# The second layer of the third and fourth expert in high and low parts, in a three-stage kernel on one core

## The chip, the cores and the metric

The kernel runs on one core of one Trainium2 chip. The metric is the device time of one execution in microseconds (us). Inputs and outputs lie in the chip's memory; the launch is one program. An engine is named as the profile names it: PE is TensorE, DVE is VectorE, ACT is ScalarE, POOL is GpSimd, SP is SyncE.

## The reference

Three stages follow one another. Only the third is touched here.

```python
# 1: attention, 2 batches x 8 heads x 768 tokens x 64, masked by equal hash buckets
# 2: dense layer pair on the 1536 x 512 result
h = np.maximum(x @ w_in, 0.0)            # w_in 512 x 2048
x = h * h @ w_out                        # w_out 2048 x 512
# 3: eight experts with a greedy, capacity-limited assignment
logits = x @ w_gate                      # 1536 x 8
order = np.argsort(-logits.flatten())
for idx in order:                        # best (token, expert) pair first
    tok, e = idx // 8, idx % 8
    if assigned[tok] >= 0 or counts[e] >= 192: continue
    assigned[tok] = e; counts[e] += 1
for e in range(8):
    mask = assigned == e                 # 192 tokens each
    h = np.maximum(x[mask] @ w1[e], 0.0) # w1[e] 512 x 1024
    out[mask] = h @ w2[e]                # w2[e] 1024 x 512
```

All of it is in 32-bit floats. The greedy loop fixes one expert after the other: when an expert is full, its 192 tokens are known, and the remaining tokens go on.

## The kernel before

The three stages are written as lists of operations with their engine, an assumed duration, their dependencies, the buffers they take and give back, and a priority. A planner (`Sched`) puts them in one order per engine before the program is built; the order is then fixed, and each engine works through its own list from front to back. Buffers are units of named pools (`UNITS_F`), and the planner gives an operation its unit when one is free.

The third stage is `experts`. Expert number p (0 to 7) is the p-th one that the router finishes, so "the third and fourth expert" are p = 2 and p = 3. For each expert:

- the router (`rank`, `rest`, `front`, `squeeze`, `slots`) finds the 192 tokens. It is a chain of short operations on DVE and PE: comparison tables (L1342 on DVE) are counted on PE (L1349), DVE reads the counts (L1385 to L1389), PE transposes a vector twice (L1394, L1400), DVE picks the expert and its tokens, PE makes running sums (L1140, L1143) and the token list (L1468), and DVE writes the list (L1472);
- `before` gathers the tokens' rows on the POOL queue (L1647) and transposes them on PE (L1665, L1667); SP reads the expert's number and loads its weights in four parts g = 0 to 3 (L1610 a quarter of w1, L1611 a quarter of w2) into one of 12 units of the pool `raw`;
- `add1` runs the first layer of a part on PE (L1703, 8 matrix products of 192 columns) and the rectifier, on ACT or DVE;
- `add2` runs the second layer of that part. It has two forms. For p below `HP` the product is made of 32-bit numbers: 8 products of 192 columns for each part (L1744) into a transposed result, which two products with zeros have opened (L1750), which is copied out (L1803 ACT, L1805 DVE), transposed back on PE (L1812) and copied once more (L1819 ACT, L1821 DVE). For p of `HP` and above `add2r` is used: w2 and the rectified h are each split into a high part of the reduced type fp32r and the rest, and three products of parts replace the full one.

```python
nc.scalar.activation(wh(p, g, 0), w, AF.Copy)                                                   # L1621, high part of w2
nc.vector.tensor_tensor(wh(p, g, 1), w, wh(p, g, 0).bitcast(F32), op=OP.subtract)               # L1623, low part
nc.scalar.activation(h[:, :, 0:192], abank(n), AF.Relu)                                         # L1714, high part of h
nc.vector.scalar_tensor_tensor(..., 0.0, h[:, :, t].bitcast(F32), op0=OP.max, op1=OP.subtract)  # L1717, low part, two pieces
# add2r, for each of the 8 slices of 128 rows of an expert's w2, 512 columns each:
nc.tensor.matmul(o, h[:, 0:128], w, ...)      # L1772   tokens 0 to 127: high x high
nc.tensor.matmul(o, h[:, 0:128], wl, ...)     # L1773   high x low
nc.tensor.matmul(o, h[:, 256:384], w, ...)    # L1774   low x high
nc.tensor.matmul(o, h[:, 128:256], w, ...)    # L1776   tokens 128 to 191: high and low rows x high
nc.tensor.matmul(o[0:64], h[:, 128:192], wl, ...)  # L1779  high x low
```

Here the result has the tokens in its rows, so nothing is transposed back: ACT copies (L1835, L1839) and DVE adds (L1837). The split halves of w2 lie in the pool `wh`, which has two units; a part of h lies in one of three units of `hr` (`hx` for the other form). A `raw` unit goes back when its first layer is done and, for the split form, its w2 is split; for the other form when the second layer has read it. The result of an expert takes the pool `S`, which has one unit left for it. Last, POOL scatters the rows to the output (L1826).

The first layer of a part has priority 24.5, the second layer in the 32-bit form 70.5 and in the split form 20, the splits of w2 50; the smaller number goes first among what is ready.

Of the kernel before, what the change touches and what calls it, by code (L numbers as in the profile page):

```python
# [1577 lines left out]

FP = {"ga": 27, "xp": -0.5, "xe": -35.5, "m1": 24.5, "re": -38, "m2": 70.5, "ye": -30, "yt": -20, "yo": -40.5, "sc": -10.5, "sp": 50, "mr": 20}
AP = 5  # L1580
HP = 4
RSLACK, ESLACK = 0, 0.2
PSLACK = 0.15
SC = 2.2
# [8 lines left out]
def experts(tc, nc, S, ps, mem, ident, router, x2d, w1, w2, out, L, cst, slot):  # L1593
# [12 lines left out]
    def weights(p, g, v):  # L1606
# [7 lines left out]
        WD[p, g] = d = S.add("DMA", 3.7, None, [s], prio=p, lat=1.8)  # L1614
        if p < HP:
            return
# [79 lines left out]
    def add1(p, g):  # L1696
# [29 lines left out]
        T["l1", n] = a  # L1726
        if p >= HP:
            S.add("NONE", 0.0, None, [a, WS[p, g]], rel=[("raw", T["ld", p, g])])
# [8 lines left out]
    def add2(p, g):  # L1737

        n = 4 * p + g
        if p >= HP:  # L1740
            return add2r(p, g, n)
# [24 lines left out]
    def add2r(p, g, n):  # L1766

        def mm(j, b):
            w, wl = (wh(p, g, i)[:, 512 * j:512 * j + 512] for i in range(2))
            h, o, z = hx(n)[:, j], yr(p)[b], (g, j) == (3, 1)  # L1770
            if b == 0:
                nc.tensor.matmul(o, h[:, 0:128], w, start=(g == j == 0), stop=False)  # L1772
                nc.tensor.matmul(o, h[:, 0:128], wl, start=False, stop=False)  # L1773
                nc.tensor.matmul(o, h[:, 256:384], w, start=False, stop=z)  # L1774
            else:
                two = lambda: nc.tensor.matmul(o, h[:, 128:256], w, start=(g == j == 0), stop=z)  # L1776
                if not z:
                    two()
                nc.tensor.matmul(o[0:64], h[:, 128:192], wl, start=False, stop=False)  # L1779
                if z:  # L1780
                    two()

        a = T.get(("l2d", n - 1))
        js = [(j, b) for j in range(2) for b in (1, 0)] if g < 3 else [(j, b) for b in (1, 0) for j in range(2)]
        for i, (j, b) in enumerate(js):
            first = (g, i) == (0, 0)
            a = S.add("PE", MMR * (2 if b else 3), lambda j=j, b=b: mm(j, b), [WS[p, g], HD[n], a], prio=FP["mr"], acq="S" if first else (),
                      rel=[("hr", T["h", n]), ("wh", T["wh", p, g])] if i == 3 else ())
            if first:
                T["y", p] = a  # L1790
            T["l2", p, b] = a
        T["l2d", n] = a

    def after(p):
# [38 lines left out]
        def yr_ev(h):  # L1833
            if h == 0:
                nc.scalar.activation(yo(0), yr(p)[0], AF.Copy)  # L1835
            elif h == 1:
                nc.vector.tensor_tensor(yo(1), yr(p)[1][0:64], yl(), op=OP.add)  # L1837
            else:
                nc.scalar.activation(yl(), yr(p)[1][64:128], AF.Copy)  # L1839
# [5 lines left out]
        ev = []  # L1845
        if p >= HP:
            T["yl", p] = l = S.add("ACT", .6, lambda: yr_ev(2), [T["l2", p, 1]], prio=FP["yo"], acq="yl")
# [105 lines left out]
```

## Time and profile before

| what | value |
|---|---|
| median of 3 runs | 794.07 us (793.15 to 800.98) |
| the profiled execution's own time | 795.63 us |
| its span, first to last instruction | 793.9 us |
| mean granted PE clock | 0.989 of full speed |
| PE busy | 769.3 us, 97% of the span |
| DVE, ACT, POOL busy | 526.6, 414.1, 385.8 us |

Times within the trace count from the start of the span. The experts begin at about 577 us and the last scatter at 789. A matrix product of 32-bit numbers is two records of PE, since the program issues it in two passes. Durations of PE's records overlap; what a record costs PE in a dense run is the distance from one start to the next. An engine's idle time has cost only where the engine is the one that the end waits for.

### The profile page before, as it was taken

Reading aid. Unit: us, or ns where it says so; the run is one execution under the profiler, and the core shown is the slowest. Engines: PE = TensorE matmul, PEld = TensorE weight load, DVE = VectorE, ACT = ScalarE, POOL = GpSimd, SP = SyncE. Lnnn points to the kernel's source line nnn. Section 1 sums busy time; section 2 is a strip of 40 time slices with the busy share of each in tenths; the row PEclk is TensorE's granted clock in tenths of the full one; section 3 lists DMA queues with packets and bytes.
Section 4 is the critical chain, followed back from the end, with each engine's and each line's share of the span. In section 5 each row is a group of like instructions: output and inputs, shape, how many; then the busy total and the mean of one; then the engine's idle time right before and its main releaser. Section 6 shows DMA issues by size and latency. Waiting matters only on the chain.

```text
span 793.9 us, 14029 instructions
## 1 busy us (share of the span) xinstructions
PE 769.3 (97%) x5087; PEld 680.7 (86%) x5087; DVE 526.6 (66%) x1100; ACT 414.1 (52%) x825; POOL 385.8 (49%) x395
## 2 busy tenths in 40 slices
PE   8999999999988999999999999999999999999996
PEld 5788888988977889889989999998589998898885
DVE  6888988989998856733861791347967778413432
ACT  6989999999977754532442433244402312103432
POOL 2767877877896745752672473148400212311211
PEclk9999999999999999999999999999889999999999
DMA  8959648655721033310330110202265778667100
GB/s 189 235 134 197 131 104 182 136 123 128 185 73 54 1 107 107 107 53 1 107 107 1 53 54 1 80 1 81 68 220 180 249 248 282 211 226 258 41 21 20
DMA packets 87973, 94.34 MB, mean 119 GB/s; under 512 B 41920, under 2 KB 66880, under 8 KB 87904
## 3 DMA queue, kind: packets, MB, share of 16 engines
q1 hardware_dynamic: 85856, 87.16, 38.8%
q0 software_dynamic: 2048, 6.29, 2.5%
q8 instruction: 40, 0.66, 0.3%
q14 instruction: 29, 0.24, 0.1%
HBM read 63.55 MB, written 6.29 MB: 88 GB/s over the span
## 4 chain that ended last, share of the span: by engine, by line
PE 79%; issue 9%; DVE 5%; POOL 3%; ACT 2%; DMA 1%; SPq 0%; POOLq 0%; ACTq 0%; DVEq 0%
PE psTP L787 15%; PE psS L814 11%; PE psS L563 8%; PE psS L1703 8%; PE psS L1744 5%; PE psTP L599 3%; PE psO L814 3%; PE psm L814 3%; PE psTP L620 2%; PE psO L599 2%; PE psTP L621 2%; PE psm L599 2%; PE psm L620 1%; POOL out_dram L1826 1%; DVE p L611 1%
## 5 line engine op out<-in xcount | busy, mean ns | idle before, releaser
L591 POOL TENSOR_TENSOR f<-f 128x768 f32<-128x768 f32 x96 | 143.4, 1497 | 32.0 <-PE psTP L599 14.6
L800 POOL TENSOR_TENSOR r<-f,r 128x384 fp32r<-128x384 f32 x64 | 86.1, 1353 | 100.0 <-ACT r L798 95.2
L787 PE MATMUL psTP<-r 128*128 128x384 f32 x732 | 133.6, 336 | 1.1 <-DVE f L796 1.1
L787 PEld LDWEIGHTS psTP<-r 128*128 128x128 f32 x732 | 128.2, 188 | 3.8 <-DVE f L796 1.4
L796 DVE TENSOR_TENSOR f<-f,psTP 128x384 f32<-128x384 f32 x61 | 33.3, 552 | 108.3 <-ACT f L794 108.2
L814 PE MATMUL psS<-r 128*128 128x512 f32 x384 | 96.7, 396 | 0.0
L579 DVE TENSOR_REDUCE f<-psS 128x1 f32<-128x768 f32 x96 | 90.6, 947 | 5.3 <-PE psS L563 3.8
L582 ACT ACTIVATE f<-psS,f 128x768 f32<-128x768 f32 x96 | 87.0, 907 | 3.9 <-POOL f L591 1.8
L563 PE MATMUL psS<-r 128*128 128x384 f32 x384 | 87.4, 349 | 0.8 <-ACT f L582 0.8
L814 PEld LDWEIGHTS psS<-r 128*128 128x128 f32 x384 | 70.6, 188 | 13.2 <-POOL r L800 0.3
L1703 PE MATMUL psS<-ff,rf 128*128 128x192 f32 x400 | 79.6, 341 | 1.0 <-DVE rf L1707 0.9
L794 ACT ACTIVATE f<-psTP 128x384 f32<-128x384 f32 x61 | 30.1, 494 | 88.3 <-PE psTP L787 84.0
L563 PEld LDWEIGHTS psS<-r 128*128 128x128 f32 x384 | 65.2, 188 | 4.7 <-ACT f L582 1.8
L1703 PEld LDWEIGHTS psS<-ff,rf 128*128 128x128 f32 x400 | 66.7, 195 | 2.3 <-DVE rf L1707 1.6
L1826 POOL DMA_INDIRECT out_dram<-ff,ix x16 | 15.7, 982 | 100.5 <-DVE ff L1837 54.9
L1647 POOL DMA_INDIRECT ff<-x2d,ix x16 | 18.3, 1146 | 91.4 <-DVE ix L1472 67.5
L611 DVE TENSOR_TENSOR p<-psTP,p 128x384 fp32r<-128x384 f32 x102 | 55.3, 548 | 3.4 <-ACT p L607 2.6
L607 ACT ACTIVATE p<-psTP 128x384 fp32r<-128x384 f32 x102 | 49.8, 500 | 14.6 <-PE psTP L599 13.6
L599 PE MATMUL psTP<-ident,f 128*128 128x128 f32 x306 | 51.0, 278 | 1.8 <-DVE p L611 1.5
L777 POOL TENSOR_TENSOR r<-f,r 128x1024 fp32r<-128x1024 f32 x16 | 40.5, 2530 | 23.3 <-ACT r L775 23.3
L798 ACT ACTIVATE r<-f 128x384 fp32r<-128x384 f32 x64 | 33.2, 527 | 27.0 <-DVE f L796 27.0
L599 PEld LDWEIGHTS psTP<-ident,f 128*128 128x128 f32 x306 | 38.8, 143 | 8.0 <-issue 2.1
(411 smaller groups left out, 1630.2 us busy)
## 6 DMA issues: line engine op xcount, KB each, us to landing
rf<-in_moe_w_dram SPq DMA_DIRECT2D x60, 512.0 KB, 4.5
r<-r SPq DMA_DIRECT2D x90, 192.0 KB, 4.2
f<-in_moe_w_in_dram SPq DMA_DIRECT2D x16, 512.0 KB, 4.1
f<-in_moe_w_out_dram SPq DMA_DIRECT2D x16, 512.0 KB, 4.6
r<-r SPq DMA_DIRECT2D x15, 384.0 KB, 3.8
f<-in_q_dram SPq DMA_DIRECT2D x8, 384.0 KB, 5.2
f<-in_k_dram SPq DMA_DIRECT2D x8, 384.0 KB, 5.8
f<-in_v_dram SPq DMA_DIRECT2D x8, 384.0 KB, 4.5
```

Source lines behind the costliest of these rows:

```text
L563: nc.tensor.matmul(sbank(u)[:, hf, 0:384], T["q", (pr, h)][:, n, 128 * i:128 * i + 128], T["k", (pr, h)][:, n, 384 * hf:384 * hf + 384], s ...
L579: nc.vector.tensor_reduce(col(0, u), sbank(u)[:, :, 0:384], axis=AX.XY, op=OP.max, negate=True)
L582: nc.scalar.activation(P(u).rearrange("p (a b) -> p a b", a=2), sbank(u)[:, :, 0:384], AF.Exp, bias=col(0, u), accum_out=col(1, u))
L591: nc.gpsimd.tensor_tensor(Pn(u), P(u), col(3, u).to_broadcast([128, 768]), op=OP.mult)
L599: nc.tensor.transpose(tp(u, g)[:, j], Pn(u)[:, 128 * c:128 * c + 128], ident)
L607: nc.scalar.activation(th, tp(u, g), AF.Copy)
L611: nc.vector.tensor_tensor(tl, tp(u, g), th.bitcast(F32), op=OP.subtract)
L777: nc.gpsimd.tensor_tensor(lo, F, hi.bitcast(F32), op=OP.subtract)
L787: nc.tensor.matmul(hbank(s, hf), w[:, c], y[:, x, sl], start=(c == 0 and i == 0), stop=(c == 3 and i == 2))
L800: nc.gpsimd.tensor_tensor(hl[:, sl], r, hh[:, sl].bitcast(F32), op=OP.subtract)
L814: nc.tensor.matmul(abank(i), a[:, t], w, start=(f == RUNS[r][1][0] and j == 0), stop=(f == RUNS[r][1][-1] and j == 2))
L1703: nc.tensor.matmul(abank(n)[:, j], raw(p, g)[:, 0, 256 * c + 128 * j:256 * c + 128 * j + 128], xT(p)[:, c], start=(c == 0), stop=(c == 3))
```

## The change

One constant, the number of the first expert whose second layer is of high and low parts:

```diff
 AP = 5
-HP = 4
+HP = 2
 RSLACK, ESLACK = 0, 0.2
```

`HP` is read in four places: where the weights are loaded (the splits L1621 and L1623 are added), in `add1` (rectifier in two parts instead of one), in `add2` (which form) and in `after` (how the result leaves). With it the third and fourth expert take the form that the fifth to eighth already have. PE's 128 products of L1744 become 64, the 32 transposes of L1812 16 and the 8 products with zeros of L1750 4; each of L1772, L1773, L1774, L1776 and L1779 grows from 32 to 48. On DVE, L1623 grows from 16 to 24, L1717 from 32 to 48 and L1837 from 4 to 6, while L1707 falls from 8 to 4 and L1805 and L1821 from 4 to 2 each. On ACT, L1621 and L1714 grow from 16 to 24 each. The loads and their sizes stay.

The planner makes a new order from the second expert's end on. Two places carry the prediction. The first is DVE while the router makes the fourth expert's token list (q, key, h, pk and mv are its small vectors, ff_5250 and ff_5251 belong to its packing, ff_5226 and ff_5227 are the halves of the third expert's second quarter of w2, rf_5215 its first part of h). The piece of the difference, with - for before and + for the change:

```order
-L1422 TENSOR_TENSOR q<-psm,mm 128x18
+L1821 COPY ff_5236<-psTP_60 64x512
 L1437 TENSOR_REDUCE ei<-ev 128x1
 L1516 TENSOR_SCALAR ff_5250<-L_98 128x72
+L1518 TENSOR_SCALAR ff_5250<-L_98 128x72
+L1422 TENSOR_TENSOR q<-psm,mm 128x18
+L1623 TENSOR_TENSOR ff_5227<-rf_5213,ff_5226 128x1024
 L1423 SCALAR_TENSOR_TENSOR q<-q 128x18
```

A split of w2 now stands between two steps of the router's chain, and the copy L1821 in front of them; a little further down, two pieces of L1717 stand ahead of the token list's L1472.

The second place is PE where the fifth expert's tokens are transposed (L1665, L1667; ff_5231 holds the gathered rows). Before:

```order
L1744 MATMUL psS_5720<-rf_5218,rf_5211 128x192
L1394 MATMUL psTP_60<-ident,X 8x128
L1703 MATMUL psS_5261<-ff_5234,rf_5204 128x192 x2
L1812 MATMUL psO<-ident,ff_5229 128x128 x2
L1812 MATMUL psm<-ident,ff_5229 64x128 x2
L1400 MATMUL psTP_60<-ident,xm 128x8
L1665 MATMUL psTP_61<-ident,ff_5231 128x128 x2
L1667 MATMUL psTP_61<-ident,ff_5231 128x64 x2
```

With the change:

```order
L1744 MATMUL psS_5720<-rf_5219,rf_5211 128x192
L1394 MATMUL psTP_60<-ident,X 8x128
L1812 MATMUL psTP_61<-ident,ff_5229 128x128 x2
L1812 MATMUL psm<-ident,ff_5229 64x128 x2
L1400 MATMUL psTP_60<-ident,xm 128x8
L1776 MATMUL psS_5720<-ff_5224,rf_5215 128x512
L1779 MATMUL psS_5720<-ff_5225,rf_5215 64x512
L1772 MATMUL psS_5719<-ff_5224,rf_5215 128x512
L1773 MATMUL psS_5719<-ff_5225,rf_5215 128x512
L1774 MATMUL psS_5719<-ff_5224,rf_5215 128x512
L1665 MATMUL psO<-ident,ff_5231 128x128 x2
L1667 MATMUL psO<-ident,ff_5231 128x64 x2
```

The second layer of the third expert now begins before the fifth expert's transposes, and the first-layer products that stood between the router's steps have moved ahead of this place. Counted from the start of the experts to the first of these transposes, PE's list held 98 products of L1703 and 64 of L1744 before; now it holds 104 of L1703, 64 of L1744 and 5 of the split form. To the fourth expert's transposes it held 79 and 41, and now 82 and 43. To the sixth expert's it held 128 and 92, and now 128, 64 and 60 of the split form.

## Rows read from the trace of the kernel before

**Rows 1.** Page, parts 1 and 2: busy us, share and instructions; tenths in 40 slices.
```profile
span 793.9 us, 14029 instructions
PE 769.3 (97%) x5087; PEld 680.7 (86%) x5087; DVE 526.6 (66%) x1100; ACT 414.1 (52%) x825; POOL 385.8 (49%) x395
```

**Rows 2.** Windows of the experts: busy us (instructions) per engine, PE clock, DMA share, GB/s.
```profile
577.00:662.00 85.00, 84.89 (x872) 78.84 (x872) 59.95 (x225) 17.53 (x30) 12.77 (x17) 0.96 0.65 222
662.00:722.00 60.00, 58.21 (x435) 54.76 (x434) 23.32 (x96) 8.10 (x15) 10.81 (x17) 1.00 0.73 244
722.00:787.00 65.00, 64.09 (x331) 55.17 (x332) 28.01 (x46) 25.39 (x36) 8.43 (x16) 1.00 0.21 73
```

**Rows 3.** Waits of PE, 577 to 787: us in total, times, longest.
```profile
PE psS L1703 <- DVE rf L1707: 0.9, 2, 0.7
PE psS L1776 <- DVE rf L1717: 0.9, 1, 0.9
PE psm L1812 <- DVE ff L1805: 0.7, 1, 0.7
```

**Rows 4.** Timeline of PE, 32-bit form: start, us, line, tiles, records.
```profile
690.25 0.38 PE L1812 MATMUL psO<-ident,ff 128*128 128x128 f32 x2
690.47 0.38 PE L1812 MATMUL psm<-ident,ff 128*64 128x128 f32 x2
690.68 1.47 PE L1744 MATMUL psS<-rf,ff 128*128 128x192 f32 x8
...
696.02 0.49 PE L1750 MATMUL psS<-zero 128*128 128x384 bf16 x2
696.35 1.79 PE L1744 MATMUL psS<-rf,rf 128*128 128x192 f32 x10
...
713.89 1.79 PE L1744 MATMUL psS<-rf,rf 128*128 128x192 f32 x10
...
720.39 0.38 PE L1812 MATMUL psm<-ident,ff 128*128 128x128 f32 x2
```

**Rows 5.** Timeline of PE, split form, first and last of 19 starts.
```profile
753.44 0.40 PE L1779 MATMUL psS<-ff,rf 128*64 128x512 f32 x1
...
757.59 0.39 PE L1774 MATMUL psS<-ff,rf 128*128 128x512 f32 x1
```

**Rows 6.** Timeline of DVE: the kinds that grow and that shrink.
```profile
692.26 0.56 DVE L1707 TENSOR_SCALAR rf<-psS 128x384 f32<-128x384 f32 x1 [1.25 <-PE psS L1744]
692.73 0.55 DVE L1805 COPY ff<-psS 128x384 f32<-128x384 f32 x1
694.26 0.68 DVE L1821 COPY ff<-psm 64x512 f32<-64x512 f32 x1 [0.98 <-PE psm L1812]
...
727.63 0.62 DVE L1717 SCALAR_TENSOR_TENSOR rf<-psS,rf 128x128 fp32r<-128x128 f32 x2
728.57 1.23 DVE L1623 TENSOR_TENSOR ff<-rf,ff 128x1024 fp32r<-128x1024 f32 x1 [0.32 <-ACT ff L1621]
...
733.32 0.68 DVE L1837 TENSOR_TENSOR ff<-psS,ff 64x512 f32<-64x512 f32 x1
```

**Rows 7.** Timeline of ACT: a split of w2.
```profile
727.49 1.05 ACT L1621 ACTIVATE ff<-rf 128x1024 fp32r<-128x1024 f32 x1
```

**Rows 8.** Timeline of DVE: a split inside the router's chain.
```profile
660.39 1.22 DVE L1623 TENSOR_TENSOR ff<-rf,ff 128x1024 fp32r<-128x1024 f32 x1
661.54 0.20 DVE L1387 TENSOR_SCALAR Z<-psTP 128x48 f32<-128x48 f32 x1
```

**Rows 9.** Waits of DVE: us in total, times, longest.
```profile
DVE ff L1623 <- ACT ff L1621: 23.5, 13, 4.4
```

**Rows 10.** Timeline of POOL: the second gather of the fifth expert.
```profile
658.90 0.91 POOL L1647 DMA_INDIRECT ff<-x2d,ix  x1 [0.31 <-issue]
```

**Rows 11.** Timeline of PE: the transposes after it.
```profile
664.21 0.44 PE L1665 MATMUL psTP<-ident,ff 128*128 128x128 f32 x2
```

**Rows 12.** DMA issues: line, queue, xcount, us to landing.
```profile
ff<-x2d,ix POOLq DMA_INDIRECT x16, 3.7
```

## The prediction, made before the changed kernel ran

> **What bounds the kernel now.** I read the page first, then the busy times by stretch, then the waits of PE, and last the timelines around the third and fourth expert. The page gives PE 769.3 us of a span of 793.9, and the other engines 66% and less [rows 1]; that is a mean over three stages, and only the experts are touched. There PE is busy 84.89 of 85 us, 58.21 of 60 and 64.09 of 65 [rows 2]. A busy row need not mean a full engine, so the waits decide: between 577 and 787 PE's waits on the other engines come to little, 0.9, 0.9 and 0.7 us the largest [rows 3]. So in this stage the end is set by how much PE has to issue, and an operation costs what it adds to the distance between PE's starts. The granted clock is 0.96 in the first stretch and 1.00 in the two that the changed products lie in [rows 2], so prices from these need no correction.
>
> **What PE no longer does.** In the 32-bit form an expert's second layer is 32 products, 64 records. Forty of them run from 713.89 to 720.39 [rows 4]: 6.50 us, 0.1625 us a record, 10.40 us an expert. The two products with zeros cost 0.33 us (696.02 to 696.35), four transposes of the result 0.43 us (690.25 to 690.68), so all eight 0.86 us [rows 4]. Together 11.59 us an expert.
>
> **What PE does instead.** In the split form an expert has 40 products of 512 columns. Starts from 753.44 to 757.59 are 18 distances [rows 5]: 4.15 us, 0.2306 us each, 9.22 us for 40. The change saves 11.59 - 9.22 = 2.37 us an expert, **4.7 us** for both. That is small because three products of parts at 512 columns replace two passes at 192: the number of records falls only from 64 to 40, and each is longer.
>
> The Trainium skill, "TensorE: Matmul & The Clock Gate", section "Back-to-back issue gap", gives 131 ns as the sustained distance of matmuls of 512 columns. By that, 80 products would cost 10.5 us, the saving would be 12.7 us and the time 781.4. Rows 5 show 231 ns for this very form in this kernel, and the measurement decides.
>
> **What DVE and ACT get.** DVE gains 8 splits of w2 at 1.23, 8 pairs of low parts of h at 0.62 and 2 additions at 0.68, and loses 4 rectifiers at 0.56, 2 copies at 0.55 and 2 at 0.68 [rows 6]: 9.84 + 4.96 + 1.36 - 2.24 - 1.10 - 1.36 = 11.5 us. ACT gains 8 splits at 1.05 [rows 7] and smaller copies; it is busy 17.53 of 85 and 8.10 of 60 us there [rows 2], and I cost it at nothing. DVE is busy 59.95 of 85 and 23.32 of 60 us [rows 2], most of it the router's chain. It takes its list in order, so a split that stands in the chain delays the chain: before, one split of 1.22 us (660.39) already stands in front of L1387 [rows 8]. Whether this costs anything is a question of what PE has left to do.
>
> Up to the fifth expert's token list the order puts two splits and three pairs of low parts into DVE's list that were not there, 2 x 1.23 + 3 x 0.62 = 4.3 us; the rectifiers and copies of the stretch are as many as before. PE's cover: its list now has six first-layer products (two records of 0.1625 us each) and five split products more in front of the fifth expert's transposes, 6 x 0.325 + 5 x 0.2306 = 3.1 us. The gather itself had room: its second part started at 658.90 [rows 10], a gather takes 3.7 us to land [rows 12], so at about 662.6, and the transposes began at 664.21 [rows 11], 1.6 us later. So 4.7 us cover 4.3, of which some falls into DVE's idle time anyway. For the fourth expert the list has 5 products more, 5 x 0.325 = 1.6 us of cover, against two splits and one pair, 3.1 us if all of it delays the list; up to 1.5 us could lie bare here. DVE is idle for 25 of the 85 us around it [rows 2], so I take zero. For the sixth expert PE holds 60 x 0.2306 - 28 x 0.325 = 4.7 us more work in front. So I cost the router's delay at zero; if the cover were gone, it would be up to 11.5 us.
>
> **Waits.** Two of PE's waits go with the old form: the transposes' wait for the copy L1805 (0.7) and the longer of the two for a rectifier, ended by the L1707 of 692.26 (0.7) [rows 3, 6]. Two come. The first split product takes the result buffer that the second expert's copies must have left, and the first-layer products that lay between have moved away; the trace doesn't show this place, so between 0 and the copy with its neighbour on DVE, 0.55 + 0.68 = 1.2 us [rows 6]; I take the middle, 0.6. The split form's own wait was 0.9 us in four experts [rows 3], 0.45 for two. Net 1.4 - 1.05 = 0.3 us saved.
>
> **The sum** is 4.7 + 0.3 = 5.0 us. The profiled execution took 795.63 us and would take 790.6; it is 1.6 us above the median of the runs, so against the median of 794.07 the forecast is **789.1 us**, 0.6% less. The loads keep their number and size, and their buffers come free earlier, since a quarter of the weights is given back after its split; I cost them at zero because PE waited for none of them.
>
> **Rivals.** *The splits come late.* `wh` has two units, so the split of a part can begin only when the part two before it is multiplied. Its path is 1.05 on ACT and 1.23 on DVE [rows 6, 7], 2.3 us, as long as one part's ten products, 10 x 0.2306. With DVE busy 39% of the stretch [rows 2], 1.23 us become 2.0, and each of the last six parts of the two experts waits 0.8: 4.7 us, and the time is 793.8. For it: the equal pace, and DVE's own wait for ACT's half, 23.5 us in 13 times [rows 9]. Against it: the last four experts run at this pace with 0.9 us of waits in all, with first-layer products in between, which the third and fourth expert have too.
>
> *The router is held back.* If all 11.5 us land on the chain before the fifth or sixth expert's list, PE's cover of 4.7 us is used up and PE stands 6.8 us: 795.9, slower than before. It decides from the point where the list comes more than 4.7 us later. For it: rows 8, and DVE at 71% in the first stretch. The Trainium skill, "PSUM — Partial Sum Buffer", section "Engine vs sequencer instructions", says that VectorE's queue is strictly first in, first out; by that rule every split ahead of a router's step delays it in full, as the order of rows 8 bears out. Against it: only 4.3 us stand before the fifth list. If DVE also waits for ACT's half, 1.8 us a time [rows 9], at six splits, 10.8 us more come, and the time is 806.7.
>
> *The split products run denser* than rows 5, or more waits go than I count. If all waits of rows 3 went and none came, the sum would be 4.7 + 2.5, 786.9; only a shorter distance gives more. That the change does nothing is excluded by the counts of the new order.
>
> **Chances.** My forecast, between 786.5 and 791.8, 74%; late splits 13%; the router held back 8%, of which 5% beyond 1%; denser products 2%; other gains beyond 786.5 3%. The range 786.5 to 796 takes in the first rival and the nearer half of the second and leaves out about 10%. One per cent, 7.9 us, is about what a measurement of this kernel tells from no change; the runs before spread over 7.8. Faster by more than that needs less than 786.1: 4%; slower, above 802.0: 5%; the same, 91%.
>
> **What the profile should show.** 128 records of L1744 where 256 were, 48 of each split product, 0.23 us between them in the third and fourth expert; waits of PE between 577 and the end still near 3 us; the fifth expert's transposes no more than 3.1 us later than 664.21; from the fifth expert's products on everything some 5 us earlier, so the last scatter about 5 us earlier. Wrong would be: a wait of several us in front of the transposes L1665 or L1394, with DVE's splits before it (the router), or in front of L1776 for L1623 (late splits), or a distance other than 0.23.

## The result and the profile after

| | before | after |
|---|---|---|
| median, 20 runs each | 794.92 us (792.81 to 800.98) | 788.66 us (787.22 to 793.69) |
| ratio after to before, 95% interval | | 0.9917 [0.9898, 0.9936] |
| profiled execution | 795.63 us | 788.25 us |

The forecast was 789.1 us. That it lies so near is partly luck: the saving is 6.3 us by these medians where 5.0 were forecast, and the forecast had started from a median of three runs, 794.07, which is 0.85 us below that of the twenty. The page of the changed kernel, parts 1 and 2, to be held against [rows 1]:

```profile
span 786.5 us, 13922 instructions
PE 761.0 (97%) x5019; PEld 669.1 (85%) x5019; DVE 536.2 (68%) x1118; ACT 423.4 (54%) x837; POOL 385.9 (49%) x395
```

PE lost 8.3 us of busy time and DVE gained 9.6 (11.5 were forecast from single durations, which overlap their neighbours by some 0.07, 1.22 for a start distance of 1.15 in [rows 8]; for the 18 operations that DVE has more this is 1.3 of the 1.9 us), while the span fell by 7.4. The three windows of [rows 2] after:

```profile
577.00:662.00 85.00, 84.17 (x871) 78.42 (x872) 62.17 (x228) 18.57 (x31) 11.45 (x15) 0.98 0.65 218
662.00:722.00 60.00, 59.46 (x399) 50.25 (x398) 37.27 (x119) 23.61 (x35) 15.83 (x27) 1.00 0.90 310
722.00:787.00 65.00, 57.28 (x303) 49.98 (x301) 22.78 (x39) 19.58 (x29) 6.88 (x13) 0.98 0.07 24
```

In the middle window DVE (the third busy time of a row) went from 23.32 to 37.27 us, and PE is a little fuller than it was (59.46 us for 58.21). In the last one PE simply ends earlier. PE's waits from 577 to 787, in place of [rows 3]:

```profile
PE psS L1776 <- DVE rf L1717: 0.9, 1, 0.9
PE psO L1667 <- DMA ff<-x2d,ix: 0.8, 1, 0.8
PE psO L1812 <- DVE ff L1805: 0.7, 1, 0.7
PE psTP L1812 <- DVE ff L1805: 0.5, 1, 0.5
```

No wait for a split L1623 is there, none for the router. The wait for the gather's data (L1667) is not new. It is that of the first expert, ahead of all that the change moves, and the kernel before had it too, with a small one for the router, beside those of [rows 3]:

```profile
PE psO L1667 <- DMA ff<-x2d,ix: 0.8, 1, 0.8
PE psTP L1394 <- DVE X L1389: 0.2, 1, 0.2
```

The groups of PE's products from 577 to 787 (busy us, mean ns), with the changed kernel:

```profile
L1776 PE MATMUL psS<-ff,rf 128*128 128x512 f32 x48 | 21.2, 441 | 0.9 <-DVE rf L1717 0.9
L1744 PE MATMUL psS<-rf,rf 128*128 128x192 f32 x96 | 20.5, 338 | 0.0
L1772 PE MATMUL psS<-ff,rf 128*128 128x512 f32 x48 | 19.0, 396 | 0.0
L1774 PE MATMUL psS<-ff,rf 128*128 128x512 f32 x48 | 18.8, 392 | 0.0
...
L1744 PE MATMUL psS<-ff,rf 128*128 128x192 f32 x32 | 6.8, 336 | 0.0
```

96 + 32 = 128 records of L1744 and 48 of each split product. Their distance in the third expert, from PE's timeline (start, duration):

```profile
672.69 0.40 PE L1779 MATMUL psS<-ff,rf 128*64 128x512 f32 x1
...
674.53 0.39 PE L1774 MATMUL psS<-ff,rf 128*128 128x512 f32 x1
```

Eight distances in 1.84 us, 0.230 each, as in [rows 5].

**Where the time went.** I add up the distances of PE's starts from the third expert's first transposes (L1665; 625.57 before, 624.62 after) to the end of the last product's issue: 161.61 us before, 155.18 after, 6.43 less.

| PE's work, us | before | after | change | forecast |
|---|---|---|---|---|
| products L1703, L1744 and the split ones | 137.01 | 133.84 | -3.17 | -2.36 |
| transposes of the result L1812 | 3.53 | 1.95 | -1.58 | -1.72 |
| products with zeros L1750 | 0.99 | 0.33 | -0.66 | -0.66 |
| waits | 2.69 | 2.10 | -0.59 | -0.3 |
| other transposes and the router's products | 17.39 | 16.96 | -0.43 | 0 |
| sum | 161.61 | 155.18 | -6.43 | -5.0 |

The three kinds of products stand in one row because a boundary between two kinds moves some 0.14 us from the one to the other. Two records of L1744 (0.33 us) that stood behind the third expert's first transposes before stand ahead of them after, so 0.3 of the first row and of the sum is no saving. Counted from the second expert's first transposes, where both orders are still the same, PE's sum falls by 6.18 us, 2.86 of it in the products. The profiled executions differ by another 1.2 us ahead of that point, in which the change has no part: at 577 to 590 us, ahead of every moved instruction, the granted clock was 0.74 before and 0.87 after. So these two profiles, 7.4 us apart, overstate the change; the ratio gives 794.92 x 0.0083 = 6.6 us [5.1, 8.1].

### The profile page after: what moved, and what is told of

It is laid out like the page before. It is cut to its first block, busy times and chain, and to the rows that moved or that the text cites. A ratio compares the mean times of both kernels' runs of the same rounds, so it can differ in the third digit from the quotient of the medians.

```text
span 786.5 us, 13922 instructions
## 1 busy us (share of the span) xinstructions
PE 761.0 (97%) x5019; PEld 669.1 (85%) x5019; DVE 536.2 (68%) x1118; ACT 423.4 (54%) x837; POOL 385.9 (49%) x395
## 4 chain that ended last, share of the span: by engine, by line
PE 74%; issue 12%; DVE 5%; POOL 4%; ACT 3%; DMA 1%; SPq 0%; POOLq 0%; ACTq 0%; DVEq 0%
PE psTP L787 15%; PE psS L814 11%; PE psS L563 8%; PE psS L1703 5%; PE psTP L599 3%; PE psS L1744 3%; PE psO L814 3%; PE psm L814 3%; PE psTP L620 2%; PE psTP L621 2%; PE psO L599 2%; PE psm L599 2%; POOL out_dram L1826 1%; PE psm L620 1%; DVE p L611 1%
## 5 line engine op out<-in xcount | busy, mean ns | idle before, releaser
L1703 PE MATMUL psS<-ff,rf 128*128 128x192 f32 x400 | 78.1, 336 | 0.0
L1703 PEld LDWEIGHTS psS<-ff,rf 128*128 128x128 f32 x400 | 66.1, 193 | 1.2
L1623 DVE TENSOR_TENSOR ff<-rf,ff 128x1024 fp32r<-128x1024 f32 x22 | 26.9, 1223 | 31.9 <-ACT ff L1621 31.9
```

The costliest lines, as they stand in the source:

```text
L1703: nc.tensor.matmul(abank(n)[:, j], raw(p, g)[:, 0, 256 * c + 128 * j:256 * c + 128 * j + 128], xT(p)[:, c], start=(c == 0), stop=(c == 3))
```

## The experiments

Each kernel ran in five rounds beside the kernel before; ratios are to that. The kernel before had medians of 795.57 us beside hp3, hp1, hp0 and dve2, 795.01 beside pe16, nolow, dve15 and dve2p, and 794.59 beside ord24 and hp0d. Executions can differ by some 5 us in what happens before the experts, where the programs are the same: the first expert's transposes start at 576.03 in the changed kernel's profile and at 581.15 in that of hp3. So beside the ratio I give a **stage time**, read from one profile each: from the second expert's first transposes to the last scatter's start. It was 187.80 us before (601.21 to 789.01) and 181.62 after (600.01 to 781.63).

My theory: PE's work sets the stage, and what DVE was given costs nothing. The rival: the router on DVE is held up and takes back part of a larger saving.

**How the saving grows with the number of experts** (hp3, hp1, hp0).

```diff
-HP = 2
+HP = 3      # hp3: the fourth expert alone is changed
+HP = 1      # hp1: the second to fourth
+HP = 0      # hp0: the first to fourth; and in add2r:
+            if p == g == j == 0 and b == 1:
+                ps.part(unit(("y", p), "S"))
```

> Only the fourth expert changes its form (the constant is 3). If the gain is PE's work, one expert gives half: 2.4 us of records and products, and about half of the 0.3 to 0.6 us of waits, so 2.4 to 3.3 us below the kernel before, a ratio of 0.996 to 0.997. If the gain comes from the new order of the whole list and not from the cheaper form, one expert can give anything, and no share near one half is to be expected.

> The second expert takes the split form too (the constant is 1). If PE's work alone decides, 2.4 us less than with the constant 2: 7.1 to 9 us below the kernel before, a ratio of 0.989 to 0.991. If the router's chain on DVE, which gets another 5.7 us of work and gets it earlier, has no cover left, the gain stops: the time is that of the constant 2 or above it, with PE waiting for the fourth or fifth expert's tokens or for the steps L1394 and L1140.

> All eight experts take the split form (the constant is 0; the first use of the split form also opens the result's buffer). By PE's work alone 4 x 2.4 = 9.5 us and some waits below the kernel before, a ratio of 0.986 to 0.988. By the router's cover: DVE gets 23 us of work more than in the kernel before, while the router has its longest tables, and the ratio stays at 0.991 or above.

| experts changed | median, us | ratio | stage time, us |
|---|---|---|---|
| 1 (hp3) | 794.09 | 0.9960 [0.9933, 0.9987] | 184.64 |
| 2 (the change) | 788.66 | 0.9917 [0.9898, 0.9936] | 181.62 |
| 3 (hp1) | 787.49 | 0.9896 [0.9861, 0.9931] | 178.08 |
| 4 (hp0) | 782.62 | 0.9817 [0.9786, 0.9847] | (other start) |

Each expert takes 3.2, 3.0 and 3.5 us from the stage: the steps are even and the router does not take them back. hp3 and hp1 came out as expected by their ratios. hp0 came out better than expected; its interval lies clear of the changed kernel's and of hp1's, so it beats both. Its experts, from the first transposes on, are 2.0 us shorter than hp1's (200.01 for 202.02); the medians are 4.9 apart. hp1's is of six runs that spread over 5.7 us; the lowest times, 785.23 and 781.76, are 3.5 apart. Where the rest comes from stays open.

**More work for PE** (pe16).

```diff
                 nc.tensor.matmul(o, h[:, 256:384], w, ...)   # L1774
+                if p < 4:
+                    nc.tensor.matmul(o, h[:, 256:384], w, start=False, stop=False)
```

> The changed kernel with one more product (low x high, L1774 issued twice, so that this part enters the sums twice) in each of the 8 slices of the third and fourth expert: 16 more products of PE, nothing more on DVE, the other orders kept. If PE's work sets the stage, 16 x 0.2306 = 3.7 us more, 3.2 to 4.2. If the router or DVE sets it and PE has room, under 1 us more.

Median 793.33, ratio 0.9981 [0.9963, 0.9999]; stage time 185.28, which is 3.66 us more than the changed kernel's, where 16 x 0.2306 = 3.69 was expected. In PE's own sum the 16 added products take 3.69 and everything else stays the same to 0.05. The medians are 4.7 us apart, above the 3.2 to 4.2 expected; pe16's runs spread over 7.5 us, and its profile begins the experts 4.8 us later than the changed kernel's, so the stage time is the better measure here. PE has no room: each product shows in full.

**Less work for DVE** (nolow).

```diff
-                nc.vector.tensor_tensor(wh(p, g, 1), w, ..., op=OP.subtract)   # L1623
+                if p >= 4:
+                    nc.vector.tensor_tensor(wh(p, g, 1), w, ..., op=OP.subtract)
-            w, wl = (wh(p, g, i)[...] for i in range(2))
+            w, wl = (wh(p, g, i if p >= 4 else 0)[...] for i in range(2))
```

> The changed kernel with every engine's order kept, but DVE's half of the split of w2 (L1623, 8 times 1.23 us) left out for the third and fourth expert; their products read the high part in its place, so the low part of w2 is missing from the two experts' sums. DVE has 9.8 us less to do, PE as much as before. If PE's work sets the stage and DVE's added work is covered: 0 to 1.2 us less than the changed kernel (only PE's small waits for DVE go). If the router, held up by these splits, sets it: 5 to 10 us less.

Median 788.56, ratio 0.9934 [0.9904, 0.9963]; stage time 181.61, against 181.62. All eight added splits can go and nothing becomes faster: in this order they cost zero.

**More work for DVE** (dve2 and dve15; the orders stay as they are).

```diff
-                nc.vector.tensor_tensor(wh(p, g, 1), w, ..., op=OP.subtract)   # L1623
+                for _ in range(2 if p < 4 else 1):                            # dve2: twice
+                    nc.vector.tensor_tensor(wh(p, g, 1), w, ..., op=OP.subtract)
+                if p < 4:                         # dve15, instead: half of it a second time
+                    nc.vector.tensor_tensor(wh(p, g, 1)[:, 0:512], w[:, 0:512], ..., op=OP.subtract)
```

> The changed kernel, with DVE's half of the split of w2 done twice for the third and fourth expert (8 x 1.23 = 9.8 us more on DVE, the lists of the other engines unchanged). If DVE's work is covered by what PE has left to do, most of it vanishes: 0 to 3 us above the changed kernel, since the fifth expert's tokens had about 1.4 us of room and two more splits stand ahead of their list. If the router's chain is what bounds the stage, nearly all of it shows: 7 to 10 us above the changed kernel, slower than before.

> The changed kernel with a half of L1623 done a second time (512 of its 1024 columns) for the third and fourth expert: some 8 x 0.65 = 5.2 us more of DVE, the orders kept. If PE's work covers some 3 us and the rest shows, as the 6.6 of 9.8 us of dve2 would have it: 1.5 to 2.5 us above the changed kernel. If there is no cover and each piece shows in proportion: 3.5 us. If the cover is the 4.7 us that I had counted: under 1 us.

dve2: 795.31, ratio 0.9986 [0.9963, 1.0008], stage time 188.34: 6.7 of the 9.8 us show. This missed what I had put on my theory. dve15: 790.99, 0.9947 [0.9928, 0.9966], 182.73: 1.1 by the stage and 2.3 by the medians, for 5.5 us of DVE (8 times 0.693 in its trace), by the medians the first of its three cases. So the cover beyond what the order was made for is some 3 to 4.4 us: most of the first 5.5 us vanish, and of the next 4.3 nothing does, since dve2 loses 4.3 to 5.6 us more than dve15. Of dve2's 6.7 us, 4.0 are waits of PE (6.1 us from the second expert's transposes on, where the changed kernel has 2.1) and 1.7 a lower clock behind one of them. DVE's timeline of dve2 shows the place of the longest wait, in the seventh expert's list and the first step of the eighth's, L1487 (its lines are one higher than before from L1624 on, which is L1623):

```profile
694.09 0.17 DVE L1425 SCALAR_TENSOR_TENSOR alive<-key,alive 128x6 f32<-128x6 f32 x1
694.18 0.16 DVE L1448 TENSOR_SCALAR h<-key 128x6 f32<-128x6 f32 x1
694.25 2.48 DVE L1624 TENSOR_TENSOR ff<-rf,ff 128x1024 fp32r<-128x1024 f32 x2
696.64 0.16 DVE L1449 SCALAR_TENSOR_TENSOR pk<-h,key 128x6 f16<-128x6 f32 x1
696.72 0.16 DVE L1454 TENSOR_TENSOR mv<-h,tok 128x6 f16<-128x6 f32 x1
696.79 0.17 DVE L1487 CAST mm<-alive 128x6 bf16<-128x6 f32 x1
```

L1487 needs only L1425's result, but stands behind the split and begins 2.7 us after it. PE's timeline beside it (in brackets the idle time and what ended it):

```profile
691.87 3.50 PE L1704 MATMUL psS<-ff,rf 128*128 128x192 f32 x20
697.01 0.17 PE L1140 MATMUL psTP<-mm,tri 128*128 128x6 bf16 x1 [1.64 <-DVE mm L1487]
...
700.31 0.63 PE L1774 MATMUL psS<-ff,rf 128*128 128x512 f32 x1
700.74 0.63 PE L1775 MATMUL psS<-ff,rf 128*128 128x512 f32 x1
701.17 0.52 PE L1777 MATMUL psS<-ff,rf 128*128 128x512 f32 x1
```

PE stands 1.64 us, and the split products after it are 0.43 us apart instead of 0.23. The windows of this kernel say why (the third number from the end is the granted clock):

```profile
688.00:695.00 7.00, 7.00 (x48) 5.97 (x47) 6.72 (x24) 2.56 (x3) 0.75 (x1) 1.00 1.02 356
698.00:701.50 3.50, 3.50 (x15) 2.67 (x14) 2.22 (x11) 0.37 (x1) 2.10 (x3) 0.51 0.64 222
702.00:709.00 7.00, 7.00 (x43) 6.19 (x42) 3.73 (x6) 3.69 (x5) 4.98 (x7) 1.00 0.81 260
```

Half clock for some 3.5 us behind the wait costs about 1.7 us, as much as the wait itself.

**The same work in an order made for it** (dve2p, ord24). Is DVE out of time, or only out of step?

```diff
-        WS[p, g] = S.add("DVE", 1.2, lambda: split(1), ...)                    # L1625
+        WS[p, g] = S.add("DVE", 2.4 if p < 4 else 1.2, lambda: split(1), ...)
```

dve2p has this and dve2's edit; ord24 has this alone.

> As dve2 (DVE's half of the split of w2 done twice for the third and fourth expert, 9.8 us more of DVE), but the planner is told the doubled duration, 2.4 for 1.2, and makes its orders with it. If dve2 lost its 6.6 us because the orders were made for shorter splits and these stood in the router's way, most of it comes back: 0 to 3 us above the changed kernel. If DVE has no room for them in any order, the loss stays at 5 to 7 us.

> The orders of dve2p (planner told 2.4 for L1623 of the third and fourth expert), with each split done once as in the changed kernel: 9.8 us less DVE work than dve2p, PE's list the same. If DVE's work costs nothing once the order is made for it: within 1 us of dve2p, so 1 to 2 us below the changed kernel, by its order alone. If dve2p still paid for its second splits: 2 to 5 us below dve2p.

dve2p: 786.79, ratio 0.9897 [0.9879, 0.9915], stage 180.29, below the changed kernel where 0 to 3 us above it was expected. ord24: 787.03, 0.9903 [0.9865, 0.9941], 180.24, as expected. With the duration known to the planner the same 9.8 us of DVE cost nothing (0.05 us of stage between the two). The waits of dve2 and then of dve2p, from 600 to 790:

```profile
PE psTP L1140 <- DVE mm L1487: 1.6, 1, 1.6
PE psTP L1394 <- DVE X L1389: 1.4, 2, 0.8
PE psS L1777 <- DVE rf L1718: 0.9, 1, 0.9
PE psO L1813 <- DVE ff L1806: 0.7, 1, 0.7
PE psS L1780 <- DVE ff L1624: 0.6, 1, 0.6
PE psTP L1813 <- DVE ff L1806: 0.5, 1, 0.5
PE psTP L1140 <- DVE al L1531: 0.3, 1, 0.3
```

```profile
PE psS L1777 <- DVE rf L1718: 0.9, 1, 0.9
PE psS L1704 <- DVE rf L1708: 0.4, 1, 0.4
```

Both orders are also 1.3 us of stage shorter than the changed kernel's, by 0.8 us of waits and 0.5 spread over all kinds of PE's work; the intervals of the ratios overlap, so the runs alone do not prove that gain.

**The same allowance for the best version** (hp0d): hp0, with 1.8 in place of 1.2 for every L1623.

```diff
-        WS[p, g] = S.add("DVE", 1.2, lambda: split(1), ...)
+        WS[p, g] = S.add("DVE", 1.8, lambda: split(1), ...)
```

> The version with all eight experts in high and low parts (hp0), the planner told 1.8 for every L1623 instead of 1.2, so that no step of the router is planned to start right behind a split. The computation is that of hp0. If such an allowance helps as in dve2p: 1 to 2 us below hp0. If dve2p's better order was chance: within 1.5 us of hp0 on either side.

Both expectations missed: 795.15, ratio 1.0017 [0.9987, 1.0047], 12.5 us above hp0. The computation is the same; only the order differs. PE's timeline and windows of hp0d (with granted clock third from the end) from the second expert:

```profile
600.90 1.88 PE L1557 MATMUL psO<-ff,ff 128*128 128x25 f16 x12 [0.88 <-DVE ff L1543]
...
604.78 0.69 PE L1667 MATMUL psTP<-ident,ff 64*128 64x64 f32 x4 [0.55 <-DMA ff<-x2d,ix]
...
611.61 1.07 PE L1349 MATMUL psTP<-Bb,ff 128*128 128x8 bf16 x27 [1.00 <-ACT ff L1340]
```

```profile
600.00:620.00 20.00, 16.86 (x150) 14.04 (x149) 14.54 (x33) 7.45 (x12) 8.00 (x7) 0.66 0.60 198
...
680.00:700.00 20.00, 17.69 (x163) 14.37 (x162) 15.81 (x69) 7.21 (x12) 4.76 (x7) 0.91 0.52 167
```

In hp0 the clock is 1.00 in both stretches. Over the experts, from the first transposes (575.82 in hp0d, 581.14 in hp0) to the last scatter, PE waits 6.5 us in hp0d and 2.3 in hp0, 4.2 more. In the same stretch the clock below 1.00 stands for 10.2 us of lost time in hp0d (in the window 600 to 620 alone 0.34 times 20 = 6.8) and for 1.7 in hp0, 8.5 more. Some of the waits lie in the slow stretches and count in both, so the two add up to more than the 11.6 us by which its experts are longer (211.59 for 200.01); together they can account for all of it. A longer assumed duration is therefore no rule: it went with 1.3 us less of stage in ord24 and with 11.6 us more of experts here. With one order of each kind, why the one came out well and the other badly is not shown.

## Why the prediction held, step by step

- **PE bounds the experts.** Shown: 16 products more cost 3.66 us of 3.69, eight splits fewer on DVE cost 0.01.
- **The price of the two forms, 4.7 us.** The products, transposes and zeros gave 3.17 + 1.58 + 0.66 = 5.4 us, 5.1 without the two records that only moved ahead of the starting point. The prices of a dense run were right (0.230 for 0.2306); the transposes gave 0.14 less than counted. Of the 0.8 us by which the products beat the forecast, 0.3 are these two records. The other 0.5 are what the products take beyond their dense prices of 0.1625 and 0.2306, 3.8 us before and 3.3 after. The step had no term for this, and it goes at least in part with cuts of the dense runs: other pieces, the router's above all, cut the runs of the 32-bit products 43 times before and 35 times after, those of the split products once and six times. The first record after a cut often takes about 0.08 us more: in the changed kernel two records of L1744 at 660.92 are followed at 661.33, 0.41 us later, where 2 x 0.1625 = 0.325. That is an estimate from the trace; no run varied the cuts alone.
- **Waits, 0.3 us saved.** It was 0.6, and the places were others, so that this term came near by luck. The two for L1707 went (0.9), and a small one for the router (0.2). The fourth expert's wait for L1805 went as forecast, but two of its kind came at the first and second expert's transposes (0.65 at 629.95, 0.54 at 664.68), and the first split product did not wait. L1717's stayed at 0.9 and did not grow.
- **The router, costed at zero.** Right in the outcome, and shown by nolow. The fifth expert's transposes came at 666.68, 2.5 us later than [rows 11], within the 3.1 forecast, with no wait; the gather's second part [rows 10] came at 661.49:

```profile
661.49 0.91 POOL L1647 DMA_INDIRECT ff<-x2d,ix  x1 [0.31 <-issue]
...
666.68 0.38 PE L1665 MATMUL psO<-ident,ff 128*128 128x128 f32 x2
```

  The reason was only half right. I had looked for the cover above all at the fifth expert's list, and there it held even in dve2 (668.15, no wait in front). The bare places are elsewhere: the fourth expert's list, where I had left up to 1.5 us open and costed them at zero and dve2 lost 1.4, and those behind the fifth expert's, where it lost the rest. DVE at a mean of 60 to 70% has time enough; whether a split costs is settled by the place it is given, as dve2 and dve2p show with the same work.
- **The splits come late.** No wait for L1623 after. DVE itself waits longer for ACT's half, 33.0 us in 18 times where [rows 9] had 23.5 in 13, and it costs nothing.
- **Denser split products.** Refuted, 0.230 us. The Trainium skill, "TensorE: Matmul & The Clock Gate", section "Back-to-back issue gap", gives 131 ns, which does not hold for this form here. pe16 measured the price alone, 3.66 / 16 = 0.229 us.

## What to carry to other kernels

Where one engine is full, price an edit by the start-to-start distance of its instructions, count how often the order cuts its dense runs, and test the price by issuing some of them twice. Work moved to an engine that is busy two thirds of the time is free only where the fixed order has a place for it; do it once more and once less, with the order kept, and the cover is measured. A planner whose assumed durations are wrong, or happen to give another order, moved this kernel by more than the change did.

## What the runs showed of the chip that I had not expected

- A short wait can cost twice. Behind a wait of 1.64 us PE ran 3.5 us at a granted clock of 0.51, about the lower of its two levels, 1.2 GHz; in hp0d five waits of 0.3 to 1.0 us between 600.9 and 613.0 went with 0.66 over the 20 us from 600. The wait of 0.91 us near the end, which every version has, left no such mark in the products behind it: the split products that follow it in hp1 are 0.23 us apart.

```profile
774.59 0.49 PE L1776 MATMUL psS<-ff,rf 128*128 128x512 f32 x1 [0.91 <-DVE rf L1717]
...
775.39 0.39 PE L1776 MATMUL psS<-ff,rf 128*128 128x512 f32 x1
775.62 0.39 PE L1772 MATMUL psS<-ff,rf 128*128 128x512 f32 x1
```

- DVE takes its list strictly in order: in dve2 a conversion of 0.17 us stood behind a split of 2.48 us though its input was ready. The Trainium skill, "PSUM — Partial Sum Buffer", section "Engine vs sequencer instructions", says so, and the trace agrees.
- With the same order up to there, the stretch from 577 to 590 us ran at a clock of 0.74 in the kernel before and 0.87 in the changed one. The distance from the first to the second expert's transposes was 25.45 and 23.98 us, 1.5 apart. In nolow and dve15 it was 25.4, in hp3, dve2 and dve2p 23.9 to 24.1, all with this same order: in comparing two traces, such a difference is not the change's.
